# One column-mode run of p times v per attention unit, with phi(k) v inside it, and a new order of the stages

## The chip, the cores and the metric

The kernel runs on one core of a Trainium2 chip. The metric is device time of one execution in microseconds; smaller is better.

## What is computed

Two equal layers over x of 2048 rows and 512 columns, batch 1, all in float32. Each layer is attention with a memory, then a gated feed-forward network:

```
x = x + A(layernorm(x)); x = x + B(layernorm(x)); then both once more, with the same weights
A: q, k, v = x wq, x wk, x wv: 32 heads of 16; four segments of 512 rows
   for each segment s, each head:
     p     = softmax(q k^T * 0.25 + causal mask)         a_dot = p v
     a_mem = phi(q) M / (phi(q) z + 1e-6)                phi(t) = t + 1 if t > 0 else exp(t)
     o     = g a_mem + (1 - g) a_dot                     g = sigmoid(beta), per head
     M, z += phi(k)^T v, sum of phi(k)
   result: o wo
B: (silu(x w_gate) * (x w_up)) w_down, 1792 wide
```

## The kernel before

**How it is written.** The kernel records all its work as operations with an engine, a cost, reads, writes and a due time (`Program.op`), and `Program.issue` then puts them out engine by engine: a list scheduler steps through a modelled time, takes on each engine the operation that is ready and has the earliest due time, and emits it. So the order of instructions on each engine follows from the costs, from the latencies between engines (`LAT`), from the price of a change of TensorE's mode (`DRAIN`) and from the due times, which are offsets in tables (`OFF` for the parts of an attention unit, `PRE` for a layer's start, `EP`, `PAIR`, `STEP`, `WAT`, `TAT`, `FIN` for the feed-forward network). No modelled time is used in this document.

**Attention.** A layer has 4 segments x 4 groups of 8 heads x 2 halves = 32 units. A unit has 4 heads. For each group, `qk_proj` projects q and k (12 matmuls of 128x512 each, L282: three products of high and low parts of the float32 operands), splits them on POOL (L469, L471) and writes them to DRAM scratch; `load3` reads them back in the unit's layout (L508 for q, L513 for k). Then per unit:

- `mx_units`: scores for the row maxima, 16 matmuls (L531) into two PSUM banks `pmx`; VectorE masks and reduces each with one custom instruction (L538) and an accumulator read. L547 transposes the maxima, ScalarE negates them (L549), and a DMA (L550) puts them into a row of q's tile.
- `at_units`: the scores again, transposed and with the maxima in (L575, 10 blocks of 128x512 into three banks `plt`), exponentials on ScalarE (L581), the triangle of the four diagonal blocks on POOL (L585), then p times v (L603) in TensorE's column mode: four heads side by side, 32 columns each, in two runs (`pv(0)` for the first four blocks, `pv(1)` for the other six). `post` normalises on VectorE (L616 to L620) and, at a group's second half, adds the memory's part.
- `mem_update` once per group and segment (three segments): phi(k) transposed (L669), then phi(k) v in column mode (L681), then the sum into M (L685, L689). `mem_read` (L653) uses M in the next segment.

The exponentials lie in tiles `p0` (blocks 0 to 3), `p1` (four blocks) and `pc` (two), one copy of each. q's and k's split parts lie in one tile `nat`, half each. The output projection `wo_proj` (L282) and the next segment's layernorm, q, k and v projections fill TensorE between units.

**Weights.** `load_w4` (first layer, L420 to L428) and `load_w` (second) load each weight in four blocks of 128 rows and split every block into a high part (ScalarE) and a low part (VectorE).

**Feed-forward network.** Two pairs of row blocks; up and gate products by a Strassen scheme (L1005) with combinations on VectorE (L1018) and weights combined and split on POOL and ScalarE (L858 to L872), down products at L1049 with sums on VectorE (L1054).

Of the kernel before, what the change touches and what calls it, by code (L numbers as in the profile page):

```python
# [33 lines left out]
OFF = {'qe': (0.481, 1.468), 'at': (0.3, 1.1), 'mx': (-0.666, 0.16), 'lf': (-0.709, -0.318), 'mr': (0.865, 0.781), 'mu': (0.556, 0.139), 'wo': (0.263, 1.746), 'qk': (-0.342, 0.41), 'v': (-0.3, 0.518), 'lp': (0.034, 1.108)}  # L34
PRE = {'c': -1.851, 'mb': 0.212, 'lv': -1.7, 'lo': -0.87, 'gate': -1.0, 'v': -1.534, 'dv': 0.12, 'qk1': -1.2, 'mx': -1.0}
EP = {'w': -1.935, 'wn': 0.178, 'ln': -3.0, 'dn': -0.06, 'up': -2.73}
POOL_W = ""
TABLE = 1.28
DRAIN = {("full", "cols"): 0.195, ("cols", "full"): 0.095}
# [3 lines left out]
    pe=dict(pe=0.01, act=0.2, dve=0.2, sp=0.19),  # L43
    act=dict(act=0.22, dve=0.13, pe=0.27, pool=0.2, sp=0.15),
    dve=dict(dve=0.13, act=0.13, pe=0.25, pool=0.16, sp=0.12),
    pool=dict(pool=0.1, dve=0.06, pe=0.13, act=0.1, sp=0.05),
# [199 lines left out]
def infini_swiglu(ctx: ExitStack, tc: tile.TileContext, x, wq, wk, wv, wo, beta, wg, wu, wd, out,  # L246
# [17 lines left out]
    def pe(n, passes, fn, reads, writes, loads=1, mode="full"):  # L264
        o = op("pe", max(passes * n / 2400 + 0.0025 + 0.0145 * loads * (passes == 1), 0.11 * loads), fn, reads, writes)
        o.mode = mode
        return o
# [128 lines left out]
    def attention(lay, x_in, x_out, slots, T, hook):  # L396
        base = P.base
        S8 = dict(zip(("qh", "ql", "kh", "kl", "xh", "xl", "vh", "vl", "oh", "ol", "th", "tl",
                       "p0", "p1", "c0", "c1", "c2", "nat"), slots))
        W, xT, oT, XN, GRP, HLF, VT = {}, {}, {}, {}, {}, {}, {}  # L400
# [6 lines left out]
        def load_w(nm, w, tags):  # L407
            wh, wl = sb(S8[nm + "h"], T8, F32R), sb(S8[nm + "l"], T8, F32R)
            W[nm] = (wh, wl)
            for kc in range(KC):  # L410
                raw = sb(tags, [128, 512])
                dma(lambda kc=kc, raw=raw: nc.sync.dma_start(raw.ap, w[kc * 128:(kc + 1) * 128, :]), [], [raw])
                split(raw, lambda t: t, wh, wl, lambda t, kc=kc: t[:, kc, :], kc, 512)

        def load_w4(nm, w, slot):
            wh, wl = sb(S8[nm + "h"], T8, F32R), sb(S8[nm + "l"], T8, F32R)
            W[nm] = (wh, wl)
            raw = sb(S8[slot], T8)
            for kc in range(KC):
                dma(lambda kc=kc: nc.sync.dma_start(raw.ap[:, kc, :], w[kc * 128:(kc + 1) * 128, :]), [], [(raw, kc)])  # L420
                act(512, lambda kc=kc: nc.scalar.copy(wh.ap[:, kc, :], raw.ap[:, kc, :]), [(raw, kc)], [(wh, kc)],
                    sbuf=True)
                if nm in POOL_W:
                    gp(1.23, lambda kc=kc: nc.gpsimd.tensor_sub(wl.ap[:, kc, :], raw.ap[:, kc, :],
                                                                wh.ap[:, kc, :].bitcast(F32)),
                       [(raw, kc), (wh, kc)], [(wl, kc)])
                else:
                    dve(512, lambda kc=kc: nc.vector.tensor_sub(wl.ap[:, kc, :], raw.ap[:, kc, :],  # L428
                                                                wh.ap[:, kc, :].bitcast(F32)),
                        [(raw, kc), (wh, kc)], [(wl, kc)])  # L430
# [27 lines left out]
        def qk_proj(s, n, nm, tag="pj"):  # L458
            g = GRP.setdefault((s, n), {})
            if nm == "q":  # L460
                g["nat"] = sb(S8["nat"], [128, 2, 2, 512], F32R)
            ps, nat = bank(tag), g["nat"]
            a = 0 if nm == "q" else 1
            c = slice(n * 128, (n + 1) * 128)
            mm3(ps, W[nm], xT[s], range(KC), lambda t, kc: t[:, kc, c], lambda t, kc: t[:, :, kc],
                lambda kc: kc, lambda kc: None, "b")
# [21 lines left out]
        C3 = {}  # L488

        def load3(u):  # L490
# [16 lines left out]
            for j in range(2):  # L507
                dma(lambda j=j: nc.sync.dma_start(  # L508
                    cq.ap[64 * j:64 * j + 48, 2 * j:2 * j + 2].bitcast(F32),
                    g["scrq"].ap[64 * j:64 * j + 64].rearrange("(p h d) r c -> h (d r) p c", h=2, d=DH)[h]),  # L510
                    [g["scrq"]], [(cq, j)], kb=196)
            for j in range(2):
# [3 lines left out]
                    [g["scrk"]], [(ck, j)], kb=196)  # L516

        def mx_units(u):
# [4 lines left out]
            def head(p, j):  # L523
                def f():
                    for grp in ((0, 1), (2,), (3,)):
# [32 lines left out]
        PARTS = (((0, 0, 512, 0, 0),), ((1, 128, 384, 1, 0), (3, 384, 128, 1, 3), (2, 256, 256, 2, 0)))  # L558

        def at_units(u):  # L560
# [4 lines left out]

            def lt(kt, qt):
                def f():
                    b, x = BLOCKS[kt, qt]
                    if b not in f_:
                        f_[b] = sb(S8[f"p{b}"], [128, 4, 4, 128]) if b < 2 else sb("pc", [128, 2, 4, 128])  # L570
                    Pb, ps = f_[b], bank("plt", ring=3)

                    def fill():
# [8 lines left out]
                        Pb.ap[:, x].rearrange("p i c -> p (i c)"), ps.ap, AF.Exp, scale=SCALE), [ps], [(Pb, x)],  # L582
                        table="exp")
                    if kt == qt:
                        gp(0.593, lambda: nc.gpsimd.affine_select(  # L585
                            out=Pb.ap[:, x], in_=Pb.ap[:, x], pattern=[[0, 4], [1, 128]], compare_op=OP.is_ge, fill=0.0,
                            base=0, channel_multiplier=-1), [(Pb, x)], [(Pb, x)])
                return f

            def pv(k):  # L590
                def f():
# [614 lines left out]
```

## Time and profile before

| | |
|---|---|
| median of 3 runs | 1937.13 us (1933.95 to 1937.19) |
| span of the profiled execution, first to last instruction | 1931.2 us |
| mean granted TensorE clock | 0.994 |
| TensorE matmuls | 11104 records |

The profiled execution is one more than the three; its span leaves out what lies before the first and behind the last instruction. A row of a timeline or of a group names the engine, the line of the kernel, the operation, output and inputs by the program's names (`s` stands for the numbered SBUF tiles `s0` to `s17`), the shapes and the count; then times. PE is TensorE's matmul, PEld its weight load, DVE VectorE, ACT ScalarE, POOL GpSimd, SP the engine that only issues DMAs. A float32 matmul without rounding stands as two records. Matmuls overlap: the next one starts before the one before has ended, so that what a matmul costs is the distance between two starts.

### The profile page before, as it was taken

How to read it: one execution, taken by the hardware profiler on the slowest of the kernel's cores; microseconds unless marked ns; L12 is line 12 of the kernel's file. 1: busy time of each engine (PE TensorE's matmuls, PEld its weight loads, DVE VectorE, ACT ScalarE, POOL GpSimd, SP SyncE). 2: the span in 40 equal slices, each digit the busy share in tenths (PEclk: the TensorE clock that was granted, in tenths of full speed). 3: DMA queues.
4: the chain of work that ended last, by engine and by line, in shares of the span. 5: the costliest groups of instructions: out<-in, count | busy, mean ns of one | idle time of the engine just before them, and what ended most of it. 6: DMA issues, size and time to landing. Idle time of an engine off the chain costs nothing.

```text
span 1931.2 us, 32319 instructions
## 1 busy us (share of the span) xinstructions
PE 1870.8 (97%) x11104; PEld 1437.2 (74%) x11104; DVE 1406.9 (73%) x3834; ACT 873.0 (45%) x1634; POOL 905.9 (47%) x1185
## 2 busy tenths in 40 slices
PE   7999999999989999999999999999999999999999
PEld 5677677776668887788867777777766788878887
DVE  5877867778777668766777678777797756686656
ACT  4555454555624343334326555555455334333332
POOL 5333443444546553655534334444355365455461
PEclk9999999999999999999999999999999999999999
DMA  7433434456131122221364344344561321221121
GB/s 235 135 111 124 132 116 146 129 151 195 45 136 50 55 72 82 71 61 44 95 215 121 102 133 132 116 149 132 152 188 39 131 66 44 87 77 51 44 60 44
DMA packets 120819, 206.09 MB, mean 107 GB/s; under 512 B 14160, under 2 KB 43856, under 8 KB 120656
## 3 DMA queue, kind: packets, MB, share of 16 engines
q1 hardware_dynamic: 118608, 203.49, 34.8%
q8 instruction: 89, 1.46, 0.3%
q10 hardware_dynamic: 2048, 0.53, 0.1%
q14 instruction: 74, 0.61, 0.1%
HBM read 136.34 MB, written 67.11 MB: 105 GB/s over the span
## 4 chain that ended last, share of the span: by engine, by line
PE 78%; DVE 8%; issue 4%; DMA 4%; POOL 3%; ACT 2%; SPq 0%; ACTq 0%; DVEq 0%; POOLq 0%
PE pj L282 16%; PE pj L1049 14%; PE plt L1005 11%; PE pmx L531 8%; PE pmx L1005 8%; PE ppv L603 7%; PE plt L575 6%; PE ppv L1005 3%; DVE junk L538 2%; DMA ck<-scrk 1%; PE pj L975 1%; PE pj L373 1%; PE pj L653 1%; DMA s<-nm 1%; POOL mem L858 1%
## 5 line engine op out<-in xcount | busy, mean ns | idle before, releaser
L538 DVE CUSTOM_DVE_ANT_0 junk<-pmx,amask 128x128 bf16<-128x128 f32 (+3 forms) x1024 | 458.7, 484 | 116.9 <-PE pmx L531 112.0
L282 PE MATMUL pj<-s,s 128*128 128x512 f32 x1416 | 488.2, 410 | 4.9 <-DVE s L1054 4.5
L1049 PE MATMUL pj<-s,vt 128*128 128x512 f32 x1296 | 414.4, 398 | 7.1 <-DVE s L1054 4.5
L581 ACT ACTIVATE s<-plt 128x512 f32<-128x512 f32 x512 | 284.2, 601 | 141.3 <-PE plt L575 133.3
L282 PEld LDWEIGHTS pj<-s,s 128*128 128x128 f32 x1416 | 263.9, 190 | 71.4 <-issue 24.9
L531 PE MATMUL pmx<-ck,s 127*128 127x256 f32 (+2 forms) x1024 | 299.1, 347 | 16.9 <-DVE mx L538 9.5
L1005 PE MATMUL plt<-s,s 128*128 128x512 f32 x1008 | 296.2, 396 | 3.4 <-ACT tt L1020 2.3
L1049 PEld LDWEIGHTS pj<-s,vt 128*128 128x128 f32 x1296 | 243.5, 189 | 68.9 <-DVE s L1054 8.0
L1054 DVE TENSOR_TENSOR s<-s,pj 128x512 f32<-128x512 f32 x224 | 152.9, 684 | 137.9 <-PE pj L1049 137.7
L575 PE MATMUL plt<-s,ck 128*128 128x256 f32 x1280 | 241.6, 288 | 4.2 <-DMA s<-nm 2.1
L531 PEld LDWEIGHTS pmx<-ck,s 127*128 127x128 f32 x1024 | 178.7, 190 | 88.8 <-DVE mx L538 27.0
L1005 PE MATMUL pmx<-s,s 128*128 128x512 f32 x720 | 239.2, 396 | 3.6 <-ACT s L871 2.4
L575 PEld LDWEIGHTS plt<-s,ck 128*128 128x128 f32 x1280 | 211.2, 189 | 32.7 <-ACT s L581 8.5
L1005 PEld LDWEIGHTS plt<-s,s 128*128 128x128 f32 x1008 | 189.6, 189 | 50.4 <-ACT tt L1020 2.7
L585 POOL TENSOR_SCALAR_AFFINE_SELECT s<-s 128x512 f32<-128x512 f32 x192 | 126.9, 664 | 186.5 <-ACT s L581 180.1
L1005 PEld LDWEIGHTS pmx<-s,s 128*128 128x128 f32 x720 | 135.5, 189 | 36.4 <-ACT s L871 3.2
L603 PE MATMUL ppv<-s,vt 128*32 128x512 f32 (+2 forms) x1536 | 136.8, 458 | 0.0
L872 POOL TENSOR_TENSOR s<-mem,s 128x512 fp32r<-128x512 f32 x96 | 126.4, 1318 | 0.0
L469 POOL TENSOR_SCALAR s<-raw 128x512 fp32r<-128x512 f32 x64 | 39.9, 624 | 181.0 <-ACT raw L468 180.6
L1005 PE MATMUL ppv<-s,s 128*128 128x512 f32 x288 | 112.8, 394 | 0.0
L879 POOL COPY turn<-vt 128x1 f32<-128x1 f32 x20 | 3.7, 184 | 230.0 <-DVE vt L962 230.0
L581 ACT ACTIVATE pc<-plt 128x512 f32<-128x512 f32 x128 | 76.8, 600 | 63.8 <-PE plt L575 62.5
(197 smaller groups left out, 2872.5 us busy)
## 6 DMA issues: line engine op xcount, KB each, us to landing
s<-scrq SPq DMA_DIRECT2D x128, 192.0 KB, 3.5
ck<-scrk SPq DMA_DIRECT2D x128, 192.0 KB, 4.5
scrq<-s SPq DMA_DIRECT2D x32, 512.0 KB, 3.0
scrk<-s SPq DMA_DIRECT2D x32, 512.0 KB, 3.1
scrq<-s SPq DMA_DIRECT2D x32, 256.0 KB, 2.0
scrk<-s SPq DMA_DIRECT2D x32, 256.0 KB, 2.0
xin<-xmid SPq DMA_DIRECT2D x32, 256.0 KB, 2.7
s<-xmid SPq DMA_DIRECT2D x32, 256.0 KB, 5.4
```

Source lines behind the costliest of these rows:

```text
L282: pe(n, passes, lambda: nc.tensor.matmul(view(ps.ap), lhsT=av(a.ap), rhs=bv(b.ap), start=start, stop=stop), [(a, rk[0]), (b, rk[1])], [ps])
L469: gp(0.59, lambda: nc.gpsimd.tensor_scalar(out=nat.ap[:, a, 0, :], in0=raw.ap, scalar1=1.0, scalar2=0.0, op0=OP.mult, op1=OP.add), [raw], ...
L531: nc.tensor.matmul(ps.ap[:, a * 256:a * 256 + nk], lhsT=cq.ap[0:127, 2 * j + p, qt * 128:(qt + 1) * 128], rhs=ck.ap[0:127, p, 0:nk], start ...
L538: dve(w, lambda a=a, qt=qt, w=w, ps=ps, junk=junk: nc.vector.tensor_tensor_reduce(out=junk.ap[:, :w], in0=ps.ap[:, a * 256:a * 256 + w], i ...
L575: nc.tensor.matmul(ps.ap[:, 256 * p:256 * p + 256], lhsT=ck.ap[:, p, kt * 128:kt * 128 + 128], rhs=cq.ap.rearrange("r (j p) c -> r p j c", ...
L581: act(512, lambda: nc.scalar.activation(Pb.ap[:, x].rearrange("p i c -> p (i c)"), ps.ap, AF.Exp, scale=SCALE), [ps], [(Pb, x)], table="exp")
L585: gp(0.593, lambda: nc.gpsimd.affine_select(out=Pb.ap[:, x], in_=Pb.ap[:, x], pattern=[[0, 4], [1, 128]], compare_op=OP.is_ge, fill=0.0, b ...
L603: nc.tensor.matmul(ps.ap[32 * i:32 * i + 32, q0:q0 + w], lhsT=vt.ap[:, kt, VW * hd:VW * hd + 32], rhs=f_[sl].ap[:, b0:b0 + w // 128, idx], ...
L872: gp(n / 400, lambda hi=hi, lo=lo, src=src: nc.gpsimd.tensor_sub(lo(), src(), hi().bitcast(F32)), [read, (wt, (o0, 0))], [(wt, (o0, 1))])
L1005: pe(512, 1, lambda i=i, kc=kc, x=x, buf=buf, view=view: nc.tensor.matmul(ps.ap, lhsT=w.ap[:, o, i, kc], rhs=view(buf.ap, kc), start=(x == 0),
L1049: pe(512, 1, lambda i=i, j=j, fi=fi, x=x, ps=ps, wt=wt, cs=cs: nc.tensor.matmul(ps.ap, lhsT=ht.ap[:, 0:2048].rearrange("p (f a c) -> p f a ...
L1054: dve(512, lambda ps=ps, t=t: nc.vector.tensor_add(xb.ap[:, t, :], xb.ap[:, t, :], ps.ap), [ps, (xb, t)], [(xb, t)])
```

## The change

- **One run.** `pv(0)` and `pv(1)` become one `pv`, in the order of blocks (0,.), (1,.), (3,3), (2,.), behind all ten exponentials of the unit.
- **A second home.** In odd units the first four exponentials do not go to `p0`: two go to `nat`'s second half, two to a new tile `pb`. Their first run of p times v is cut in two pieces of 256 columns. So k's split parts now share `nat`'s first half with q's, except for the first two groups of a layer.
- **phi(k) v inside.** `mem_update` no longer issues L681; it puts its matmuls on a list that the next `pv` takes in, and the sum into M (`mem_add`) follows that run.
- **One `junk` tile** for L538's unused output instead of two.
- **Weights by columns.** q's and k's weights are loaded and split in four groups of 128 columns, as four times 128 columns per partition (512 bytes a piece), each with a due time of its own (`w1` to `w3`); v's and o's stay in rows. The fourth layernorm of the start is on POOL instead of ScalarE.
- **Order.** All tables of offsets, the latencies (by about 1.45), and the price of a change of mode are new; `OFF` has one table per layer.

Cut to its core:

```diff
-PAIR, STEP, WAT, TAT = 13.0, 1.83, -2.5, (-1.0, -0.5)
+PAIR, STEP, WAT, TAT = 15.838, 2.488, -12.222, (-12.051, 7.528)
-FIN = 1.9
-WQ1 = -6.0
+FIN = 17.556
+WQ1 = -21.562
...
-DRAIN = {("full", "cols"): 0.195, ("cols", "full"): 0.095}
+DRAIN = {("full", "cols"): 0.2, ("cols", "full"): 0.15}
...
-    act=dict(act=0.22, dve=0.13, pe=0.27, pool=0.2, sp=0.15),
+    act=dict(act=0.32, dve=0.19, pe=0.39, pool=0.29, sp=0.22),
...
+        def wcols(nm, w, n):
+            if nm in "qk":
+                return w[:, n * 128:(n + 1) * 128].rearrange("(k p) c -> p k c", p=128)
+            return w[n * 128:(n + 1) * 128, :].rearrange("(k p) c -> p k c", p=128)
...
-            a = 0 if nm == "q" else 1
+            a = 1 if nm == "k" and s == 0 and n < 2 else 0
...
-                            junk = sb("junk", [128, 512], BF16, ring=2)
+                            junk = sb("junk", [128, 512], BF16)
...
+            def tile_of(kt, qt):
+                b, x = BLOCKS[kt, qt]
+                if b == 0 and u % 2 and x < 2:
+                    return NAT["nat"], (1, x), lambda x=x, k=1: NAT["nat"].ap[:, 1].bitcast(F32).rearrange(
+                        "p a (i c) -> p a i c", i=4)[:, x:x + k]
+                if b == 0 and u % 2:
+                    b, x = 3, x - 2
+                if b not in f_:
+                    f_[b] = sb((S8["p0"], S8["p1"], "pc", "pb")[b], [128, 4 if b < 2 else 2, 4, 128])
+                return f_[b], x, lambda x=x, k=1: f_[b].ap[:, x:x + k]
...
-            def pv(k):
...
+            def pv():
+                ps = f_["pv"] = bank("ppv")
+                runs = (((0, 0, 2), (0, 2, 2)) if u % 2 else ((0, 0, 4),)) + ((1, 1, 3), (3, 3, 1), (2, 2, 2))
...
+                    for f, _, _ in MU_:
+                        f()
...
+                pe(1280 + 100 * len(MU_), 4, go, [(vt, c) for c in range(8)] + reads + [e[1] for e in MU_],
+                   [ps] + [e[2] for e in MU_], mode="cols")
+                for _, _, pm in MU_:
+                    mem_add(pm)
...
-            units = [lt(0, q) for q in range(4)] + [lt(1, q) for q in (1, 2, 3)] + [pv(0)]
-            units += [lt(2, 2), lt(3, 3), lt(2, 3), pv(1)]
+            units = [lt(0, q) for q in range(4)] + [lt(1, q) for q in (1, 2, 3)]
+            units += [lt(2, 2), lt(3, 3), lt(2, 3), pv]
...
-            pe(2 * VW * 4, 4, go, [pk] + [(vt, c) for c in range(8)], [pm], loads=3, mode="cols")
+            MU.append((go, pk, pm))
...
-                XN[0, t] = ln_norm(xt, lambda a: a, None, XN4, on_act=True)
-            load_w4("q", wq, "p0")
-            at(-1.95)
-            load_w4("k", wk, "p1")
-            at(PRE["lv"])
-            load_w4("v", wv, "th")
+                XN[0, t] = ln_norm(xt, lambda a: a, None, XN4, on_act=t < 3)
+            for n in range(4):
+                at((-2, PRE["w1"], PRE["w2"], PRE["w3"])[n])
+                load_w4("q", wq, "p0", (n,))
+                load_w4("k", wk, "p1", (n,))
+                if n == 0:
+                    at(PRE["lv"])
+                    load_w4("v", wv, "th")
```

More of the change, by code (lines that the diff above doesn't have):

```diff
@@ new lines, in load_w4 @@
+        def load_w4(nm, w, slot, groups=range(4)):
+            if nm not in W:
+                W[nm] = sb(S8[nm + "h"], T8, F32R), sb(S8[nm + "l"], T8, F32R)
+                RAW4[nm] = sb(S8[slot], T8)
+            (wh, wl), raw = W[nm], RAW4[nm]
+            for n in groups:
+                rv = lambda n=n: wview(nm, raw.ap, n)
+                hv, lv = lambda n=n: wview(nm, wh.ap, n), lambda n=n: wview(nm, wl.ap, n)
+                dma(lambda n=n, rv=rv: nc.sync.dma_start(rv(), wcols(nm, w, n)), [], [(raw, n)])
+                act(512, lambda rv=rv, hv=hv: nc.scalar.copy(hv(), rv()), [(raw, n)], [(wh, n)], sbuf=True)
+                dve(512, lambda rv=rv, hv=hv, lv=lv: nc.vector.tensor_sub(lv(), rv(), hv().bitcast(F32)),
+                    [(raw, n), (wh, n)], [(wl, n)])
@@ L790, in attention @@
             if w8 == LPW and s + 1 < nseg:
-                put([lambda t=t: ln_pre(s + 1, t) for t in range(4)], *OFF["lp"], 9)
+                put([lambda t=t: ln_pre(s + 1, t) for t in range(4)], *OF["lp"], 9)
             order = [e for e in items if e[1] >= 2] + [e for e in items if e[1] < 2]
```

136 lines of the change are left out of this document (63 added, 73 removed).

## The prediction

> **What bounds the kernel now.** I read the page's busy line and its chain first, then busy time by stage, then TensorE's timeline inside one attention stage.
>
> ```profile
> span 1931.2 us, 32319 instructions
> PE 1870.8 (97%) x11104; PEld 1437.2 (74%) x11104; DVE 1406.9 (73%) x3834; ACT 873.0 (45%) x1634; POOL 905.9 (47%) x1185
> ...
> PE 78%; DVE 8%; issue 4%; DMA 4%; POOL 3%; ACT 2%; SPq 0%; ACTq 0%; DVEq 0%; POOLq 0%
> ```
>
> TensorE is busy 97% and is 78% of the chain that ended last. Busy is not useful, though, since a matmul's row overlaps the next one's; the starts tell more. Two stages by themselves (the stretch and its length, then the busy time of PE, PEld, DVE, ACT and POOL, the granted clock, the DMA share, GB/s):
>
> ```profile
> 100.00:500.00 400.00, 390.05 (x2973) 290.31 (x2972) 305.74 (x1154) 211.72 (x414) 171.10 (x257) 1.00 0.46 136
> ...
> 950.00:1500.00 550.00, 535.35 (x3839) 397.70 (x3838) 419.65 (x1470) 281.76 (x542) 235.31 (x349) 0.99 0.45 134
> ```
>
> In both attention layers (100 to 500, 950 to 1500) VectorE works 76% of the time beside a full TensorE and the granted clock is whole, so time there is saved only by taking work or stalls from TensorE, and VectorE has a quarter in hand. The change's main edits lie there.
>
> **The change, part by part.**
>
> *Column runs.* p times v (L603) and phi(k) v (L681) use TensorE in column mode, 32 columns per matmul, between full-width ones. TensorE's timeline of one unit (start, duration of the group):
>
> ```profile
> 249.31 0.39 PE L282 MATMUL pj<-s,s 128*128 128x512 f32 x1
> 249.63 1.07 PE L603 MATMUL ppv<-s,vt 128*32 128x512 f32 x8
> 250.63 0.50 PE L282 MATMUL pj<-s,s 128*128 128x512 f32 x1
> 250.97 0.39 PE L531 MATMUL pmx<-ck,s 127*128 127x512 f32 x1
> ...
> 254.73 0.62 PE L282 MATMUL pj<-s,s 128*128 128x512 f32 x2
> 255.18 0.40 PE L575 MATMUL plt<-s,ck 128*128 128x256 f32 x2
> ...
> 256.25 1.07 PE L603 MATMUL ppv<-s,vt 128*32 128x384 f32 x16
> 257.13 0.61 PE L603 MATMUL ppv<-pc,vt 128*32 128x256 f32 x8
> 257.68 1.19 PE L282 MATMUL pj<-s,s 128*128 128x512 f32 x4
> ```
>
> Two L282 between 254.73 and 255.18 are 0.225 us each: the pitch inside full mode. The L282 in front of the first run takes 249.63 - 249.31 = 0.32, 0.09 over it; the one behind it 250.97 - 250.63 = 0.34, 0.11 over. The first run (512 columns of results) takes 1.00, the second (768 columns in three pieces) 257.68 - 256.25 = 1.43. The 256 further columns cost 0.43, so 512 cost 0.86 and 0.14 of the first run is fixed. Joining the two runs of a unit thus saves 0.14 + 0.09 + 0.11 = 0.34 us; 2 layers x 32 units = 64 joins: **21.8 us**. If a piece had a price of its own (the second run has three, 384, 128 and 256 wide), the 256 columns would cost less than 0.43 and the fixed part would be over 0.14, so 0.14 is the low end. The 32 odd units of the change cut their first piece in two, which I cost at nothing (upper bound: 8 more records a unit at the 0.007 us between records, 0.06 x 32 = 2 us).
>
> ```profile
> 246.12 0.46 PE L681 MATMUL pj<-vt,of 128*32 128x34 f32 x32
> 246.51 0.50 PE L282 MATMUL pj<-s,s 128*128 128x512 f32 x1
> ```
>
> phi(k) v alone is a run of 0.39 (246.12 to 246.51). Elsewhere the old order happened to put it behind the first run:
>
> ```profile
> 403.69 1.07 PE L603 MATMUL ppv<-s,vt 128*32 128x512 f32 x8
> 404.57 0.48 PE L681 MATMUL pj<-vt,of 128*32 128x34 f32 x32
> 404.98 0.67 PE L531 MATMUL pmx<-ck,s 127*128 127x384 f32 x2
> ```
>
> Both take 404.98 - 403.69 = 1.29, so it adds 0.29 and saves, inside a run, 0.10 + 0.09 + 0.11 = 0.30. In the order of instructions, the old program has 150 column runs (64 + 62 alone, 2 joined, 22 of L681 alone), the new one 64, of which 24 hold L681; so 22 x 0.30 = **6.6 us**. Both together: **-28.4**.
>
> *What the joined run waits for.* All ten exponentials and four triangle masks of a unit must be done before it, and it holds the first tiles (L581's out) until its end; hence the second home in odd units. I summed pitches over both orders: from the last score matmul (L575) of a unit to its run lie 2.15 us of TensorE work at the median before and 2.22 after; those under 2.2 us from the last masked block to the run fall short by 2.6 us in all before, 5.2 after. Behind a waiting run stand every score and projection matmul. Bounds 0 and +5; I take **+2**.
>
> *The maximum's way back.* After the maxima of a unit, L547 transposes them, ScalarE negates, and a DMA puts them beside q; then the first L575 may go.
>
> ```profile
> 53.44 0.27 PE L547 MATMUL pj<-ident,mx 128*16 128x128 f32 x1
> ```
>
> and, waiting for that DMA,
>
> ```profile
> 57.40 0.51 PE L575 MATMUL plt<-s,ck 128*128 128x256 f32 x2 [0.26 <-DMA s<-nm]
> ```
>
> That way is 57.40 - 53.44 = 3.96 us here. In the old order 7 of 64 units have less than 3.9 us of TensorE work between the two, 4.8 us short in all; in the new order 24 units, 20.3 short. The old shortfall shows up as waits of about its size:
>
> ```profile
> PE plt L575 <- DMA s<-nm: 2.1, 3, 1.0
> ```
>
> Bounds 0 (another stall lies in between) and +15.5; I take +9, over half, since most of the new shortfalls are under half a microsecond.
>
> *One junk buffer instead of two.* Each masked maximum (L538) now waits for the one before it: the order has 1728 VectorE waits on itself, 1316 before. What such a wait costs is in two pairs of rows:
>
> ```profile
> 258.57 0.25 DVE L617 RECIPROCAL r<-tt 128x16 f32<-128x16 f32 x1
> 258.86 0.23 DVE L618 TENSOR_SCALAR r<-r,gnot 128x16 f32<-128x16 f32 x1
> ```
>
> ```profile
> 1424.92 0.28 DVE L538 CUSTOM_DVE_ANT_0 junk<-pmx,amask 128x128 bf16<-128x128 f32 x1
> 1425.13 0.08 DVE L538 DVE_READ_ACCUMULATOR2_ANT mx<- 128x1 f32 x1
> 1425.13 0.42 DVE L538 CUSTOM_DVE_ANT_0 junk<-pmx,amask 128x256 bf16<-128x256 f32 x1
> ```
>
> L618 needs L617 and starts 0.04 behind its end. The second maximum does not need the first's accumulator read and starts with it, 0.08 before its end. So the wait costs 0.12 us, and only where one maximum follows another directly: 680 times in the old order, 536 in the new. 536 x 0.12 = 64 us of VectorE, over some 950 us of attention: 76% becomes 83%, no bound by itself. It reaches TensorE through the two score banks, whose waits now are
>
> ```profile
> PEld pmx L531 <- DVE mx L538: 27.0, 53, 1.3
> PE pmx L531 <- DVE mx L538: 9.5, 23, 1.1
> ```
>
> Bounds 0 and +64. The new order spreads a unit's score matmuls wider (median 11.3 us of TensorE work from first to last, 9.4 before), so I stay near the low end: **+4**.
>
> The Trainium skill, "VectorE: DVE Perf Modes", section "The DRAIN you can't avoid", has eight copies take the same time with a semaphore behind each and behind the last alone. By that the term would be 0 instead of +4; the rows above disagree (0.04 behind an end against 0.08 before it).
>
> *The start.* q and k weights now come by groups of 128 columns, two groups of each ahead of x. Now:
>
> ```profile
> 13.31 7.10 PE L282 MATMUL pmx<-s,s 128*128 128x512 f32 x19 [0.68 <-ACT s L377]
> ```
>
> and the first score matmul:
>
> ```profile
> 42.53 1.08 PE L531 MATMUL pmx<-ck,s 127*128 127x256 f32 x3 [3.15 <-DMA ck<-scrk]
> ```
>
> SP's queue ahead of it, and the bandwidth of the first 30 us in 40 slices:
>
> ```profile
> 34.46 0.43 SPq L348 DMA_DIRECT2D xin<-in_A_x_dram  x1
> 34.98 1.79 SPq L513 DMA_DIRECT2D ck<-scrk  x4
> ```
>
> ```profile
> GB/s 0 0 49 339 339 224 303 371 388 322 358 393 404 388 412 407 399 364 136 1 1 1 6 42 212 315 405 412 391 260 330 93 390 358 292 14 396 311 0 22
> ```
>
> DMA moves near 390 GB/s once it runs. 1 MB of weights ahead of x delays x by 1 MB / 390 GB/s = 2.7 us, at half rate for the 512-byte pieces 5.4; the first L282 moves from 13.3 to 14 or 15, of which I take 15 (the fourth row tile goes to POOL, which unloads ScalarE). But the 24 matmuls of the first q and k then find their weights split: now 19 of them take 7.10 where 19 x 0.23 = 4.4, and SP's queue held the loads of k (34.98) behind an x load that waits for a buffer (34.46). In the new order q's loads pass x; k's still stand behind it. By then about 89 matmuls, 20.5 us, lie ahead of the first score: 15 + 20.5 + 1.5 for the value weights, which now stand behind wo on SP, is 37, with 2.3 us of work moved behind it: 42.5 - 37 - 2.3 = 3. Bounds -7 and +3; I take **-3**.
>
> The Trainium skill, "DMA: Bandwidth & Descriptors", section "Specifications", puts full line rate at 512 bytes and above. By that the 2.7 holds, not the 5.4: 14 instead of 15, and the term would be -4. No row of this case shows pieces of that size alone.
>
> *The feed-forward stages.* Their instructions are the same; only due times change (WAT from -2.5 to -12.2 loads the first products' weights far earlier). Two such waits can go:
>
> ```profile
> PE pmx L1005 <- ACT s L871: 2.4, 2, 2.1
> ```
>
> With the stalls at the stage's start and middle I bound it by -10 and +6 and take **-5**.
>
> Sum: -28.4 + 2 + 9 + 4 - 3 - 5 = **-21**. The profiled execution spans 1931.2; the median of the runs is 1937.1 and the fastest 1934.0, so 3 to 6 us lie around the span or between executions, and the change touches none of that. 1937.1 - 21 = **1916 us**, span 1910.
>
> **The rivals.**
>
> *A. The runs' saving comes and the new order also closes stalls.* The score banks get more distance (1.64 to 1.80 us at the median between a bank's two uses), and the waits terms (+15) are hidden by the work in between: -28.4 - 3 - 10, some **1896**. For it: VectorE's and ScalarE's slack. Against: 24 short ways back instead of 7.
>
> *B. The gain is eaten by waits.* All of the 15.5 for the way back, 5 for the run, 12 for the junk wait: -28.4 + 32.5 - 3 is about zero: **1937**.
>
> *C. Slower: the score chain becomes the limit.* With one junk buffer, the L538 sequence runs at 0.12 us more each; where TensorE has nothing but score matmuls left, every one is a stall. The other terms come to -28.4 - 3 - 5 + 9 + 2 = -25, so it decides from 25 us, 40% of the 64, on. At three quarters exposed (48): 1937 - 25 + 48 = **1960**. Against: 112 us of L538's idle time now end by a matmul, so much of the wait falls where VectorE waits anyway.
>
> ```profile
> L538 DVE CUSTOM_DVE_ANT_0 junk<-pmx,amask 128x128 bf16<-128x128 f32 (+3 forms) x1024 | 458.7, 484 | 116.9 <-PE pmx L531 112.0
> ```
>
> *D. The runs don't save.* If the fixed 0.14 belongs to each piece and not to entering the mode, and the longer run drains as long as two, then at most 7 of the 28.4 come, and with the other terms (-8 and +15) it is 1937 - 7 - 8 + 15 = **1937**. Against: L681 cost 0.29 inside a run and 0.39 alone, so something is paid once per run.
>
> **How the numbers follow.** Forecast (1905 to 1927) 0.50; A (1885 to 1905) 0.22; B and D (1927 to 1945) 0.16; C (over 1945) 0.12. A measurement of this kernel can tell 0.2%, 4 us, from no change. B and D split 0.08 faster, 0.05 same, 0.03 slower. Faster 0.80, same 0.05, slower 0.15. The range, 1893 to 1940, leaves out a part of A and all of C.
>
> **What would show it.** One L603 run per unit, of 2.28 us alone and 2.57 with L681 in it, 0.09 before and 0.11 behind: right. Idle of L575 behind DMA s<-nm near 15 us: the way back; L538 starting 0.04 behind each accumulator read, and L531 waiting for mx far over 36 us: C. First score before 40 us: the start. It would be wrong if stalls in attention grow by over 28 us or the feed-forward stages, which hold half the span, change by more than 10.

## The result and the profile after

The changed kernel takes 1924.9 us (median of 5 runs, 1919.1 to 1928.8) against 1937.1 (1933.8 to 1937.9): ratio 0.9943, 95% interval 0.9926 to 0.9961. The forecast was 1916, with 0.80 on faster. One execution of run 1 below took 6319 us, far outside the rest, and is left out. Lines have moved: L283 is the old L282, L545 the old L531, L552 L538, L561 L547, L597 L575, L624 L603, L706 L681, L1035 L1005 and L1079 L1049; in the experiments they lie a few lines further on.

The page of the profiled execution after (the slowest of the five) begins:

```profile
span 1927.1 us, 33037 instructions
...
PE 1848.0 (96%) x11360; PEld 1448.9 (75%) x11360; DVE 1433.0 (74%) x3834; ACT 884.1 (46%) x1633; POOL 910.1 (47%) x1186
```

Busy time of the first attention stretch, columns as in the prediction:

```profile
100.00:500.00 400.00, 387.87 (x3170) 303.01 (x3169) 327.09 (x1191) 218.74 (x425) 171.33 (x265) 1.00 0.47 137
```

VectorE's share went from 76% to 82% there: 1191 instructions instead of 1154, and the maxima overlap less, since each now waits for the one before it (over the whole span L552 is busy 495.5 us where L538 was 458.7, at 484 ns each in both). TensorE's timeline has the joined runs, first a unit without phi(k) v, then one with it:

```profile
207.24 0.50 PE L545 MATMUL pmx<-ck,s 127*128 127x256 f32 x2
207.67 1.93 PE L624 MATMUL ppv<-s,vt 128*32 128x512 f32 x24
...
209.96 0.45 PE L545 MATMUL pmx<-ck,s 127*128 127x384 f32 x1
...
221.48 0.64 PE L624 MATMUL ppv<-s,vt 128*32 128x256 f32 x8
...
223.66 0.48 PE L706 MATMUL pj<-vt,of 128*32 128x34 f32 x32
224.07 0.68 PE L545 MATMUL pmx<-ck,s 127*128 127x256 f32 x3
```

209.96 - 207.67 = 2.29 and 224.07 - 221.48 = 2.59: the forecast had 2.28 and 2.57. The second unit is an odd one, whose first piece is cut in two; that costs nothing that shows. The waits of TensorE that grew or were expected to grow (us in total, times, longest):

```profile
PE plt L597 <- DMA s<-nm: 13.7, 14, 2.3
PE pmx L545 <- DVE mx L552: 12.9, 29, 0.8
...
PE ppv L1035 <- ACT s L901: 2.8, 2, 1.5
```

The same for its weight loads:

```profile
PEld pmx L545 <- DVE mx L552: 19.3, 46, 1.1
PEld plt L597 <- DMA s<-nm: 19.2, 15, 2.6
```

The maximum's way back (L597 behind nm, the negated maxima) went from 2.1 and 3.6 to 13.7 and 19.2; the wait for maxima, 9.5 and 27.0 before, hardly moved (12.9 and 19.3). That row alone would have cleared the junk buffer; run 5 shows that it costs about 7 us.

**Where the time went.** I added up TensorE's timeline: each interval from one start to the next, less the pitch that this shape has without a wait (0.230 for 512 columns, 0.14 + 0.09 + 0.11 for a run's edges, and so on). The pitches alone come to 1771.7 us before and 1742.9 after: -28.8. The rest is stalls (time in which the next matmul starts later than the pitch), and a part that the forecast did not have: stretches at half clock. Windows of the kernel before (granted clock third from the end):

```profile
42.60:49.20 6.60, 6.09 (x17) 4.81 (x18) 4.77 (x21) 0.00 (x0) 1.42 (x3) 0.50 0.92 328
544.40:547.60 3.20, 3.20 (x9) 2.42 (x9) 2.54 (x5) 1.14 (x2) 0.00 (x0) 0.50 0.46 164
783.30:786.50 3.20, 2.97 (x7) 2.39 (x8) 3.03 (x5) 1.31 (x3) 3.20 (x5) 0.50 0.54 164
978.00:984.50 6.50, 5.12 (x12) 4.05 (x13) 2.69 (x6) 0.00 (x0) 1.07 (x2) 0.50 0.93 249
1732.20:1735.50 3.30, 2.92 (x7) 1.82 (x6) 1.50 (x2) 1.63 (x3) 3.30 (x4) 0.50 0.58 159
```

and of the kernel after:

```profile
779.50:782.70 3.20, 3.20 (x9) 2.42 (x9) 1.86 (x4) 1.10 (x2) 3.20 (x4) 0.50 0.06 22
1281.20:1284.40 3.20, 3.20 (x13) 2.81 (x12) 2.38 (x9) 1.47 (x3) 0.68 (x2) 0.50 0.25 89
```

Five such stretches before, two after; the first 5 us of projections, which have the same slow pace in both kernels (see the start, below), stand among the stalls of the first row. The mean granted clock is 0.994 and 0.998, so 0.006 x 1931.2 = 11.6 and 0.002 x 1927.1 = 3.9 us of clock are missing; by the pitches of the matmuls inside these stretches it is 11.1 and 3.7. With that taken out, the stalls by stage (us):

| stage | before | after |
|---|---|---|
| to the first score matmul | 11.8 | 7.3 |
| attention, layer 1 | 46.0 | 57.5 |
| feed-forward, layer 1 | 24.3 | 24.3 |
| attention, layer 2 | 40.2 | 57.3 |
| feed-forward, layer 2 | 15.5 | 17.7 |

The first matmul starts at 12.27 instead of 6.65 (+5.6). So the spans of the two profiles differ by -28.8 (pitches) - 7.4 (clock) + 5.6 (first matmul) + 26.4 (stalls) = -4.2; measured 1927.1 - 1931.2 = -4.1. The medians differ by more, -12.3, since the profile after is the slowest of its runs and the one before lies at the fast end of its own. Where the 26 us of stalls come from is what the experiments ask.

### The profile page after: what moved, and what is told of

It reads as the page before. It is cut to its first block, busy times and chain, and to the rows that moved or that the text cites. A ratio compares the mean times of both kernels' runs of the same rounds, so it can differ in the third digit from the quotient of the medians.

```text
span 1927.1 us, 33037 instructions
## 1 busy us (share of the span) xinstructions
PE 1848.0 (96%) x11360; PEld 1448.9 (75%) x11360; DVE 1433.0 (74%) x3834; ACT 884.1 (46%) x1633; POOL 910.1 (47%) x1186
## 5 line engine op out<-in xcount | busy, mean ns | idle before, releaser
L552 DVE CUSTOM_DVE_ANT_0 junk<-pmx,amask 128x128 bf16<-128x128 f32 (+3 forms) x1024 | 495.5, 484 | 98.4 <-PE pmx L545 43.4
L283 PE MATMUL pj<-s,s 128*128 128x512 f32 x1416 | 476.1, 404 | 3.5 <-DVE raw L989 1.4
L1079 PE MATMUL pj<-s,vt 128*128 128x512 f32 x1296 | 405.9, 397 | 3.6 <-DVE s L1084 2.7
L603 ACT ACTIVATE s<-plt 128x512 f32<-128x512 f32 x448 | 255.9, 604 | 202.2 <-PE plt L597 181.9
L1035 PE MATMUL plt<-s,s 128*128 128x512 f32 x1008 | 320.6, 395 | 8.7 <-ACT s L970 4.0
L545 PE MATMUL pmx<-ck,s 127*128 127x256 f32 (+2 forms) x1024 | 301.4, 344 | 20.2 <-DVE mx L552 12.9
L1079 PEld LDWEIGHTS pj<-s,vt 128*128 128x128 f32 x1296 | 242.8, 188 | 67.0 <-DVE s L1084 5.8
L283 PEld LDWEIGHTS pj<-s,s 128*128 128x128 f32 x1416 | 258.8, 189 | 41.5 <-DVE raw L989 2.3
L597 PE MATMUL plt<-s,ck 128*128 128x256 f32 x1280 | 249.3, 288 | 15.0 <-DMA s<-nm 13.7
L597 PEld LDWEIGHTS plt<-s,ck 128*128 128x128 f32 x1280 | 220.5, 190 | 47.8 <-DMA s<-nm 19.2
L1035 PE MATMUL pmx<-s,s 128*128 128x512 f32 x720 | 242.8, 395 | 0.0
L1035 PEld LDWEIGHTS plt<-s,s 128*128 128x128 f32 x1008 | 189.2, 188 | 57.2 <-ACT s L970 6.8
L545 PEld LDWEIGHTS pmx<-ck,s 127*128 127x128 f32 x1024 | 177.9, 189 | 71.7 <-DVE mx L552 19.3
L1035 PEld LDWEIGHTS pmx<-s,s 128*128 128x128 f32 x720 | 135.1, 188 | 31.2
L1035 PE MATMUL ppv<-s,s 128*128 128x512 f32 x288 | 113.6, 397 | 2.8 <-ACT s L901 2.8
L624 PE MATMUL ppv<-s,vt 128*32 128x384 f32 (+3 forms) x1536 | 115.7, 419 | 0.0
L479 POOL TENSOR_SCALAR s<-raw 128x512 fp32r<-128x512 f32 x64 | 40.6, 634 | 140.3 <-ACT raw L478 137.7
L624 PEld LDWEIGHTS ppv<-s,vt 128*32 128x32 f32 x1536 | 43.4, 109 | 65.1 <-issue 50.5
```

Source lines behind the costliest of these rows:

```text
L283: pe(n, passes, lambda: nc.tensor.matmul(view(ps.ap), lhsT=av(a.ap), rhs=bv(b.ap), start=start, stop=stop), [(a, rk[0]), (b, rk[1])], [ps])
L479: gp(0.59, lambda: nc.gpsimd.tensor_scalar(out=nat.ap[:, a, 0, :], in0=raw.ap, scalar1=1.0, scalar2=0.0, op0=OP.mult, op1=OP.add), [raw], ...
L545: nc.tensor.matmul(ps.ap[:, a * 256:a * 256 + nk], lhsT=cq.ap[0:127, 2 * j + p, qt * 128:(qt + 1) * 128], rhs=ck.ap[0:127, p, 0:nk], start ...
L552: dve(w, lambda a=a, qt=qt, w=w, ps=ps, junk=junk: nc.vector.tensor_tensor_reduce(out=junk.ap[:, :w], in0=ps.ap[:, a * 256:a * 256 + w], i ...
L597: nc.tensor.matmul(ps.ap[:, 256 * p:256 * p + 256], lhsT=ck.ap[:, p, kt * 128:kt * 128 + 128], rhs=cq.ap.rearrange("r (j p) c -> r p j c", ...
L603: act(512, lambda: nc.scalar.activation(view().rearrange("p x i c -> p (x i c)"), ps.ap, AF.Exp, scale=SCALE), [ps], [(Pb, key)], table="exp")
```

## The experiments

Times come from 5 rounds beside the kernel before; ratios are to it. Apart from the operations that an edit moves, all but the replanned ones (6, 7, 9) keep the order of their parent on every engine. Edits are shortened to their core (... marks what is left out), with comments added.

**1. The joined run cut again.** After the first pieces of a run, the next TensorE operation goes first.

```
+ half(False)                # pieces of key block 0
+ def rest():
+     half(True)             # the other pieces
+     for f, _, _ in MU_:    # phi(k) v
+         f()
+ P.rest = rest
...
  o.fn()                     # the next TensorE operation
+ if rest:
+     rest()
```

> The changed kernel, in its own order of instructions, with each joined run cut in two again: the pieces that read key block 0, then the next TensorE operation of the order (full mode), then the other pieces (with phi(k) v where the unit has it). Only the place of one operation per unit changes. Theory (joining saves 0.14 fixed + 0.09 + 0.11 per run, as forecast): 64 x 0.34 = 21.8 us come back, 1924.9 + 21.8 = 1947 us, ratio to the kernel before 1.005. Rival (the fixed part belongs to each piece, not to entering column mode): only the two edges of full mode come back or less, under 13 us, 1930 to 1938 us. Second rival (the order has slack behind the run that a stall uses now): below 10 us.

Measured: 1947.5 us, ratio 1.0062 (1.0048 to 1.0076), 23 us more than the changed kernel by the ratios. The timeline shows one cut run:

```profile
257.88 0.64 PE L631 MATMUL ppv<-s,vt 128*32 128x256 f32 x8
258.34 0.61 PE L631 MATMUL ppv<-pb,vt 128*32 128x256 f32 x8
258.88 0.28 PE L565 MATMUL pj<-ident,mx 128*16 128x128 f32 x1
259.09 1.07 PE L631 MATMUL ppv<-s,vt 128*32 128x384 f32 x16
```

The first 512 columns take 258.88 - 257.88 = 1.00, as alone before, though they come in two pieces here. The pitches rise by 21.4 us over 64 units, 0.33 each. The joins are worth what was forecast, and the time follows at full size: TensorE sets the time there. The rivals with the price in each piece, or with slack behind, fall.

**2 and 3. Without the DMA of the maxima**, in both kernels.

```
- op("act", 0.1, lambda: nc.scalar.dma_start(
-     cq.ap[127:128].bitcast(F32).rearrange("o x (t c) -> o (x t) c", t=4),
-     nm.ap.bitcast(F32)), [nm], [(cq, "m")]).post = 2.2
+ op("act", 0.1, lambda: None, [nm], [(cq, "m")]).post = 2.2
```

> The changed kernel, in its own order, without the DMA that puts the negated maxima beside q (that row of q stays zero, so the exponentials are taken without subtracting the maximum: that part of the computation is left out). In the trace of the changed kernel the L597 matmuls have 33 us of idle time ended by this DMA (13.7 + 19.2). Theory (the way back of the maximum is what gives back most of the joins' gain): most of it goes, 1925 - 20 = 1905 us, range 1895 to 1912. Rival (these stalls hide others: the score banks or the exponentials are late next): under 8 us, 1917 to 1925 us.

> The kernel before, in its own order, without the same DMA (same part of the computation left out). Its trace has 5.7 us of idle time ended by it (2.1 + 3.6). Theory: 1937 - 4 = 1933 us; against the changed kernel without the DMA the difference is then 28 us, nearly the whole of the 28.4 of the column runs. Rival (the DMA costs both kernels the same): the difference between the two kernels stays at 12 us.

Measured: 1908.6 us, 0.9865 (0.9850 to 0.9879), from the changed kernel, and 1931.3, 0.9981 (0.9973 to 0.9990), from the one before. The exponentials are then taken without subtracting the maximum. The way back costs 15 us now (0.9943 - 0.9865 of 1935) and 3.7 before: **11 us** of the change's loss, give or take 4 by the intervals. A part of it may be clock: the runs without the DMA have 0.998 to 1.000, the changed kernel 0.997 to 0.998. The 33 us of idle rows were never 33 us of time: the matmul's idle time lies within that of its weight load, and both together cover 19.2 us. Between the two kernels without the DMA lie 23 us (1931.3 - 1908.6), not the 28 that the second expectation had.

Why is it late? The forecast counted TensorE's work against a fixed 3.96 us. By the traces that was a slow unit of the kernel before: its DMA took 3.3 us, and from L547's start to the landing the median is 2.8 us before (12 of 64 over 3.96) and 3.9 after (29 of 64). The DMA itself, issue to landing, before:

```profile
DMA to landing us min/median/max: 1.8/1.8/5.7
```

after:

```profile
DMA to landing us min/median/max: 1.8/3.1/7.0
```

One of the two longest waits of the first layer in the kernel after, the DMAs issued in its window (median us to landing at the end) and the matmul that waited:

```profile
scrq<-s SPq DMA_DIRECT2D x1, 512.0 KB, 7.3
s<-scrq SPq DMA_DIRECT2D x2, 192.0 KB, 4.0
ck<-scrk SPq DMA_DIRECT2D x2, 192.0 KB, 5.5
...
s<-nm ACTq DMA_DIRECT2D x1, 8.0 KB, 7.0
```

```profile
421.86 0.51 PE L597 MATMUL plt<-s,ck 128*128 128x256 f32 x2 [2.18 <-DMA s<-nm]
```

The 8 KB of nm go out beside SyncE's reloads of q and k and its write of q to the scratch. In the new order 36 of the 64 take over 2.5 us, 15 before, and 21 of the 36 have a reload of q in flight when they are issued, 20 one of k; of the 28 others 1 and 4 have. The Trainium skill, "DMA: Bandwidth & Descriptors", section "Queues, rings and completion order", says that SyncE and ScalarE each have a queue row on the same 16 engines and that an engine serves the rows in turn, packet by packet. The rows agree with that (1.8 us at best, 7.0 beside these); no run here held the reloads back alone.

**4. One junk buffer in the kernel before.**

```
  tag = b.tag if b.slot is None else f"{b.tag}_{b.slot}"
+ tag = "junk" if tag.startswith("junk") else tag
```

> The kernel before, in its own order, with both junk buffers in one place, so that each masked maximum that directly follows another waits for it (680 such pairs). Theory (0.12 us each on VectorE, 82 us in all, nearly all of it where VectorE waits for scores anyway): +3 us, 1940 us, range 1936 to 1945. Rival (the wait is what gives the gain back: VectorE's chain of maxima is on the path): +12 us or more, 1949 us and over. By the rule that a semaphore costs nothing beside VectorE's own drain: 1937.

Measured: 1985.1 us, 1.0258 (1.0245 to 1.0271): **+50 us**, far over the +3. VectorE's timeline with one buffer:

```profile
301.20 0.69 DVE L539 CUSTOM_DVE_ANT_0 junk<-pmx,amask 128x512 bf16<-128x512 f32 x1
301.81 0.08 DVE L539 DVE_READ_ACCUMULATOR2_ANT mx<- 128x1 f32 x1
302.04 0.29 DVE L539 CUSTOM_DVE_ANT_0 junk<-pmx,amask 128x128 bf16<-128x128 f32 x1
302.26 0.08 DVE L539 DVE_READ_ACCUMULATOR2_ANT mx<- 128x1 f32 x1
302.37 0.42 DVE L539 CUSTOM_DVE_ANT_0 junk<-pmx,amask 128x256 bf16<-128x256 f32 x1
```

and with two (run 5):

```profile
302.59 0.69 DVE L557 CUSTOM_DVE_ANT_0 junk<-pmx,amask 128x512 bf16<-128x512 f32 x1 [0.38 <-PE pmx L550]
303.20 0.08 DVE L557 DVE_READ_ACCUMULATOR2_ANT mx<- 128x1 f32 x1
303.29 0.29 DVE L557 CUSTOM_DVE_ANT_0 junk<-pmx,amask 128x128 bf16<-128x128 f32 x1
303.50 0.08 DVE L557 DVE_READ_ACCUMULATOR2_ANT mx<- 128x1 f32 x1
303.50 0.42 DVE L557 CUSTOM_DVE_ANT_0 junk<-pmx,amask 128x256 bf16<-128x256 f32 x1
```

From maximum to maximum 0.84 and 0.33 instead of 0.70 and 0.21: 0.12 to 0.14 each, the forecast's 0.12. What was wrong was the assumption that VectorE waits there anyway. 680 x 0.13 = 88 us on VectorE and 50 of them reach TensorE; by its starts, stalls ahead of score matmuls grow from 37.2 to 78.1 us. By the Trainium skill, "VectorE: DVE Perf Modes", section "The DRAIN you can't avoid", where eight copies take no longer with a semaphore behind each, it would be 1937; for a maximum and the accumulator read behind it the rows and the time say otherwise.

**5. Two junk buffers in the changed kernel.**

```
+ if tag == "junk":                       # two homes in turn
+     self.turn = not getattr(self, "turn", False)
+     tag = f"junk_{int(self.turn)}"
+ elif tag[:3] in ("nm_", "tur"):         # makes room
+     tag = tag[:-1] + "0"
```

> The changed kernel, in its own order, with two junk buffers in turn as before (the memory comes from giving the negated maxima and the one-element turn buffer one home each). Theory from the run that gave the kernel before one buffer (+50 us, of which 41 in stalls ahead of score matmuls; in the changed kernel those stalls are only 7 us over the kernel before): the new order hides most of the wait, two buffers save 3 to 10 us, 1925 - 6 = 1919 us. Rival (the one buffer costs the new order as much per direct follower, 536/680 of 50 = 39 us): 1886 us. Second rival (nothing left to save): 1924 us and over.

Measured: 1916.6 us, 0.9906 (0.9887 to 0.9925): **7 us** faster than the changed kernel by the ratios, give or take 5 by the intervals, the best single edit that leaves nothing out. It also takes away the second home of the negated maxima, so that the buffer alone may be worth a little more. The new order hides most of the wait, not all.

**6 and 7. Code and order crossed.** The changed code with all numbers of the old planner (OFF, PRE, EP, PAIR, LAT, DRAIN and the rest), and the old code with all of the new.

```
- PAIR, STEP, WAT, TAT = 15.838, 2.488, -12.222, (-12.051, 7.528)
+ PAIR, STEP, WAT, TAT = 13.0, 1.83, -2.5, (-1.0, -0.5)
...
+ PRE.update(w1=-2, w2=-2, w3=-2)
```

> The changed kernel's code (one run per unit, phi(k) v in it, one junk buffer, weights by columns) with all due times, latencies and mode prices of the kernel before. Theory (the new order is what carries the one junk buffer and the longer hold of the first tiles): the column runs still save 28, the one buffer costs up to 50 as in the run on the kernel before, so 1937 - 28 + 40 = 1949 us, range 1930 to 1960, with stalls ahead of score matmuls far over 44 us. Rival (the order is worth nothing by itself): 1920 to 1928 us.

> The kernel before (two runs per unit, phi(k) v by itself, two junk buffers, weights by rows) with all due times, latencies and mode prices of the changed kernel. Theory (the order alone saves nothing on column runs; it makes the way back of the maxima short): about the kernel before plus 5 to 15, 1945 us, with idle time of the score-transposed matmuls behind the DMA of the maxima over 15 us. Rival (the new order is itself a gain): under 1935 us.

Measured: 1944.8 us, 1.0041 (1.0029 to 1.0053), and 1958.3, 1.0113 (1.0098 to 1.0128). With one buffer in the code and two in the old one, neither half gains: code without order loses 8 us, order without code 22 (the forecast had 5 to 15); together they gain 11 to 12. The landing of nm in the first of these two

```profile
DMA to landing us min/median/max: 1.8/1.8/4.5
```

speaks against the forecast's way of counting: by TensorE's work 26 of its units are short of 3.9 us, 23.5 us in all, about as in the new order, and yet the matmuls of L597 (L598 there) idle only 2.3 and 3.2 us behind the DMA. With much the same work in between, it is the landing that differs.

**8. The old order, joined runs, two junk buffers** (edit 5 on the code of run 6).

> The changed kernel's code planned with all due times of the kernel before (that run took 1944.8 us with one junk buffer), the same order, with two junk buffers in turn. Theory (what kept that order slow is VectorE's wait on the one buffer): stalls ahead of score matmuls fall from 63 to about 40 us, 1945 - 23 = 1922 us, range 1912 to 1930; then the joined runs alone gain about 14 us on the old order and the new order little by itself with two buffers. Rival (the old order is slow with joined runs for another reason, the longer hold of the first tiles): 1938 us and over.

Measured: 1921.7 us, 0.9931 (0.9918 to 0.9944). One buffer cost that order 21 to 23 us (by the ratios, and 1944.8 - 1921.7); with two, the new code gains 13 us in the old order. With two buffers the new order is worth about 5 us more (1916.6), little over what the intervals can tell, with one 20: it is above all a way to live with one buffer. Run 4 lost 50 us by the one buffer, in an order that was planned for two; planned for one and with the new code, the same due times lose 21 to 23. Which of the two takes back the rest was not tried apart.

**9 and 10. A longer booking for the DMA** (the planner counts 3.7 us), with one and with two junk buffers.

```
-     nm.ap.bitcast(F32)), [nm], [(cq, "m")]).post = 2.2
+     nm.ap.bitcast(F32)), [nm], [(cq, "m")]).post = 3.7
```

> The changed kernel with one number of its planner changed: the time that the planner books for the DMA of the negated maxima after its issue, 3.7 us instead of 2.2. The whole order is planned anew; in it 3 units have under 3.9 us of TensorE work on the way back of the maximum, 1.9 us short in all, instead of 24 units and 20.3 us. Score banks and runs come out somewhat tighter (by the same kind of sum 3 to 6 us). Theory (the way back gives back about 11 us): idle time behind that DMA falls from 33 to under 10 us, time 1924 - 7 = 1917 us, range 1911 to 1923. Rival (any new order costs as much as it saves): 1922 us and over.

> The same new order (3.7 us booked for the DMA of the negated maxima, planned with one junk buffer) with two junk buffers in turn in the program, the memory found as in the run with two junk buffers. Theory (way back and one junk buffer are separate terms of 7 to 11 and 7 us): 1924 - 7 - 7 = 1910 us, range 1903 to 1916. Rival (they cover for each other, so that the second saves nothing): 1916 us and over.

Measured: 1929.0 us, 0.9966 (0.9953 to 0.9980), and 1917.9, 0.9901 (0.9886 to 0.9916). Both miss their range. With one buffer the waits for the DMA are gone, but those for maxima took their place:

```profile
PE pmx L545 <- DVE mx L552: 17.4, 44, 1.5
...
PE plt L597 <- DMA s<-nm: 0.5, 2, 0.3
```

By TensorE's starts, stalls ahead of L597 fall by 18 us and those ahead of score matmuls rise by 9, the rest lies in small ones. My theory fails here: taking the way back out of the path is worth 15 us when nothing else moves (run 2) and nothing when the whole order is planned anew, with longer waits for maxima. In that order two buffers are worth 11 to 13 us, more than the 7 of run 5.

**11 and 12. The start.** First only x ahead on SyncE's queue.

```
  load_rows(xt, x_in, t * 128)
+ P.early.append(P.ops[-1])
...
+ for o in self.early:       # ahead of the planned order
+     o.fn()
```

> The changed kernel, its own order on all engines but SyncE, whose queue issues the four loads of x ahead of the first weight groups. Theory (the first TensorE work, at 12.3 us against 6.7 before, waits for x behind 1 MB of weights): first transposes at 7 us and the first projections a few us earlier, 1925 - 4 = 1921 us. Rival (the weights arrive later by what x gained and are what the first projections and scores wait for): first transposes early, first score matmul still at 41 us, 1925 us.

Measured: 1926.0 us, 0.9946 (0.9934 to 0.9958), no difference that shows; and the first matmul came later, at 15.3 us, the first score matmul at 44.7. VectorE's timeline says why:

```profile
8.46 0.69 DVE L445 TENSOR_TENSOR s<-s,s 128x512 fp32r<-128x512 f32 x1 [4.31 <-ACT s L444]
...
11.17 0.69 DVE L445 TENSOR_TENSOR s<-s,s 128x512 fp32r<-128x512 f32 x1 [0.21 <-ACT s L444]
11.78 0.69 DVE L360 BATCH_NORM_STATS2 bst<-tt 128x6 f32<-128x512 f32 x1
```

The planner had put four weight remainders (L445, the low parts) ahead of the statistics of x (L360); with x first, the weights came later, and the statistics stood behind them although x had landed from 3.3 us on. So the last run moved the whole normalization of x ahead on every engine, on top of run 5.

```
+ P.early = sorted(P.ops[first:], key=lambda o: o.eng != "sp")   # loads and normalization of the four tiles
...
+ for o in self.early[:4]:   # the loads, ahead of all
+     emit(o)
...
+ for x in self.early[4:]:   # the rest, right behind the constants
+     emit(x)
```

> The run with two junk buffers in the changed kernel's order (1916.6 us), with x loaded first and the whole normalization of the first four row tiles (VectorE's statistics, GpSimd's steps, ScalarE's scaling) put ahead of the four weight groups that the planner had put before it on each engine. Theory (the first transposes wait for VectorE, which has four weight remainders, 2.8 us, and their arrival in front of the statistics; that is why x alone ahead made the start 3 us later): first transposes at 7 to 8 us instead of 12, first score matmul 2 to 4 us earlier than 40.6, time 1916.6 - 3 = 1914 us. Rival (the weights are then what the projections wait for): first transposes early, first score matmul at 40 to 41 us, 1916 to 1918 us. Second rival (what the start gains or loses is taken back in the first stage, as the 3 us later start cost the other run only some 1 us): first score matmul earlier, time 1916 us and over.

Measured: 1917.5 us, 0.9911 (0.9891 to 0.9931), the same as run 5. TensorE's timeline:

```profile
7.05 1.11 PE L390 MATMUL plt<-ident,xn 128*128 128x128 f32 x4 [7.05 <-ACT xn L379]
...
14.44 1.12 PE L390 MATMUL ppv<-ident,xn 128*128 128x128 f32 x4 [2.31 <-POOL xn L382]
16.23 4.21 PE L299 MATMUL pmx<-s,s 128*128 128x512 f32 x9 [0.68 <-ACT s L394]
```

The first transposes start at 7.05, but the fourth row tile, which the change gave to GpSimd, is ready only at 14.4, and the first projection starts at 16.23 (16.31 in run 5). The first score matmul stays at 40.9 (40.6), as the first rival had it.

## Why the prediction was right, and where not

*Column runs, -28.4.* Right: -28.8 by the pitches, and cutting the runs again costs 23.

*What the joined run waits for, +2.* Nothing to see: stalls ahead of the runs (L603, now L624) are 1.3 us before and 1.4 after.

*The maximum's way back, +9.* Size about right, 11; mechanism half right. The fixed 3.96 us failed: it was a slow unit's, and the DMA lands at 3.1 us instead of 1.8 at the median. That the new order issues it beside the reloads is the likely reason (21 and 20 of the 36 late ones against 1 and 4 of the 28 others), not one that a run held alone. That the size came out is in part luck.

*One junk buffer, +4.* Measured 7 (2 to 12), on the side of the low end. The price of 0.12 held; the reason given for the low end (VectorE waits anyway) did not, since the old order pays 50 of its 88 us. Planning for one buffer, and then the new order, saved it: 50, 21 to 23 and 7 us in runs 4, 8 and 5. Rival C names the right mechanism: with the old order and the new code about half of its 48 us came (run 6, 1944.8).

*The start, -3.* Wrong: the first score matmul came at 41.4 instead of 42.5, not at 37, with 2.2 us of work moved behind it, so +1. Two steps failed. The first is "15 us for the first L282": it came at 16.6. By the traces the four tiles of x landed at 8.1 to 10.6 us, behind the four weight groups, instead of 3.5 to 6.7, and the first projection moved 3.3 us with them; run 12 shows that VectorE's and GpSimd's part holds it at 16.2 even when x comes first. Neither of the two rates weighed there held: the groups of 256 KB in 512-byte pieces land 0.90 us apart (7.90 to 14.20, run 12), the blocks of 256 KB in 2 KB rows 0.65 (7.35 to 11.86, before): 291 against 407 GB/s. So the full rate at 512 bytes, by which the term would have been -4, does not show here, nor does half of it, and 1 MB takes 3.6 us.

The second step is the reading of the 7.10 us for 19 matmuls as weights that are not yet split. Two timelines of the kernel before, then one of the kernel after:

```profile
13.31 5.48 PE L282 MATMUL pmx<-s,s 128*128 128x512 f32 x12 [0.68 <-ACT s L377]
...
18.60 1.81 PE L282 MATMUL pmx<-s,s 128*128 128x512 f32 x7
```

```profile
16.62 5.06 PE L283 MATMUL pmx<-s,s 128*128 128x512 f32 x11 [0.68 <-ACT s L378]
```

Behind the first, the matmuls up to 18.60 start 0.427 us apart and those behind it 0.23; in the kernel after the pace is the same up to 21.48. It is the pace of the half-clock stretches (six L1079 from 779.66 to 782.22 in the kernel after: 0.427 each), and no granted clock is on record before 18.65 and 21.61. So 2.5 us before and 2.3 us after go to the pace, and weights that come sooner could not win them.

*Feed-forward, -5.* What lies over the pitches there fell by 3.8, but not through waits: stalls rose by 2.2 and the loss in half-clock stretches fell by 6.0. The waits that should go stayed: the products still wait for the same weights, L1035 for L901, 2.8 us in 2 where L1005 for L871 was 2.4 in 2.

*What the sum had not:* -7 in the profiles (6 of them in the feed-forward stages, counted above), about -10 by the median clocks (0.993 and 0.998 of 1930 us), from fewer half-clock stretches; and about 10 us more of small stalls in attention (28.6 in the table, less 11 and 7), ahead of projections and transposes above all, which no run took apart. The two errors nearly cancel, which is luck. So the sign rests on the runs' saving, but the measured time came near the 1916 for a reason that the prediction did not have; without the clock it would have been 1932 to 1935.

The best versions of these runs that compute everything are the changed kernel with two junk buffers, with the longer booking or without, 0.9901 and 0.9906 of the kernel before; the intervals do not tell them apart.

## What to carry to other kernels

Before a buffer is dropped, look for what follows on the same engine: a wait of 0.13 us behind each small operation is nothing in a busy share and 50 us in time where that engine paces the bank that TensorE needs. A small DMA on the path has no fixed length, 1.8 to 7.0 us here: count what other queues have in flight when it goes out. And when an order is set anew, change code and order apart as well as together: here each alone lost, and a second buffer showed that what the code lost in the old order came from its one buffer.

## What the runs showed of the hardware

A long wait of TensorE costs more than its length. In the kernel before, all five waits over 2 us behind the start are followed by a half-clock stretch; four of their rows, beside the one of 3.15 us that the prediction shows:

```profile
543.62 1.94 PE L1049 MATMUL pj<-s,vt 128*128 128x512 f32 x5 [4.04 <-DVE s L1054]
783.53 2.08 PE L1005 MATMUL plt<-s,s 128*128 128x512 f32 x4 [2.30 <-ACT tt L1020]
979.38 1.22 PE L282 MATMUL pj<-s,s 128*128 128x512 f32 x2 [3.20 <-DVE s L1054]
1731.16 0.50 PE L1005 MATMUL pmx<-s,s 128*128 128x512 f32 x1 [2.09 <-ACT s L871]
```

Each stretch lasts 3.4 or 6.8 us and costs 1.6 to 3.2 us more. The changed kernel has more stall time but, behind the start, no wait over 2.25 us. One of its two stretches stands behind the second of these and the other behind one of 1.98 us at 778.27; none stands behind the first, nor behind the 2.18 shown above:

```profile
70.24 0.98 PE L597 MATMUL plt<-s,ck 128*128 128x256 f32 x6 [2.25 <-DMA s<-nm]
...
1280.73 0.80 PE L545 MATMUL pmx<-ck,s 127*128 127x256 f32 x3 [2.00 <-DMA ck<-scrk]
```

In each trace the half-clock stretches lie on one grid of 3.41 us. I divided the time at full clock into the windows of this grid. In the 14 traces of these kernels there are 34 windows in which TensorE's rows leave 55% or more idle, and half clock follows on all 34; it follows on 17 of the 7731 others. The wait of 2.00 us falls into one window and leaves it 59% idle; those of 2.25 and 2.18 fall across a border and leave no window more than 41% idle.

The Trainium skill, "TensorE: Matmul & The Clock Gate", section "What's actually happening", has the clock halved after an idle window of about 3.4 us on a clock that runs free of the program. The length, the half and the grid agree, and that it hits some waits and not others follows from where a wait falls; but the windows here were not idle throughout, so the traces put the point lower: 55% was always enough. Whether the shorter waits are why the changed kernel's clock is higher in all its runs was not tried by itself.
